# An exclusion between GpSimd and VectorE in a kernel's list scheduler, with updated durations

## The chip, the cores and the metric

The kernel runs on one core of a Trainium2 chip. The metric is the device time of one execution in microseconds, the median of several runs. Every run is a whole launch: inputs from HBM, all three stages, output to HBM.

## The reference

The reference chains three stages. The first is causal attention with a sliding window of 64 positions on 4 batches, 8 heads, 576 positions and 64 features a head. The other two are dense feed-forward blocks on the 2304 tokens of 512 features that come out, one after the other.

```python
scores = scale * np.matmul(q, k.transpose(0, 1, 3, 2))
mask = (rel >= 0) & (rel < window)          # window = 64
attn = softmax(np.where(mask, scores, -1e9))
x = np.matmul(attn, v)                       # -> 2304 tokens x 512

h = x @ w_in                                 # 512 -> 2048
g = h * np.clip(h + 3.0, 0.0, 6.0) / 6.0
x = g @ w_out                                # 2048 -> 512

h = x @ w2_in                                # the second block
g = np.maximum(0.01 * h, h)
out = g @ w2_out
```

## The kernel before

All matrix products keep high precision by splitting each operand into a rounded part (names that end in h) and a rest (names that end in l) and adding three products. The weights arrive as 64-bit numbers (tile st). A chain on ScalarE and VectorE turns each 128x512 block into 32-bit numbers (tile ca: lines 381, 370 twice, 386, 389 and the add that the profile calls CUSTOM_DVE_ANT_0 at line 342) and then into its two parts: w0h and w0l for the first product of a feed-forward block, w1h and w1l for the second. VectorE writes the l parts.

Attention works on items. Item 0 is one window of 64 queries, the others are pairs of windows, and each pair has two halves. For a half, TensorE computes scores into PSUM (L507). VectorE takes the row maximum (L466) and scales it into nb (L467, 128x4). ScalarE takes the exponential (L455). VectorE sums the rows (L476, in the first five items) and forms the reciprocal rc (L462 and L463, 128x4). GpSimd multiplies the probabilities by rc (L343, 128x512). TensorE transposes them (L532) and ScalarE copies the result, and TensorE multiplies by v (L564). The first five items run ahead of everything else. The later items are woven into the first feed-forward block.

That block begins with six column blocks f of 128 hidden features, over five token blocks. For each f, TensorE computes h (L617: twelve products in the order xs0h by w0h, xs0h by w0l, xs0l by w0h, then the same for xs1 to xs3), ScalarE and VectorE form g (r at L636 and L641, gh, gl at L645), and TensorE adds to y (L663). The rest of both feed-forward blocks uses a scheme with fewer products (lines from about 943 on).

The order of the work is not written by hand. The whole program is recorded in an object of class Order as a list of operations. Each operation has one or more ways (engine, modelled duration, function that emits it), the operations that it depends on, and a delay. `run` plays six rounds. A round is a forward pass, which starts the ready operation with the earliest due time on the engine that is free first, and a backward pass, which sets new due times. The round with the shortest modelled end wins, and its operations are emitted by modelled start time. Each engine then executes its own list in that order, so the modelled durations do nothing on the chip except set these lists. An operation with two ways (`copy`, `tensor_tensor`) may go to either engine, with a bias against the second way.

Of the kernel before, what the change touches and what calls it, by code (L numbers as in the profile page):

```python
# [17 lines left out]
class Order:  # L18
# [90 lines left out]
    def forward(self, due):  # L109


        ops, after = self.ops, self.after
        n = len(ops)
        left = [len(deps) + len(behind) for _, deps, behind, _ in ops]
        ready, free, done, start, used = {}, {}, [0.0] * n, [0.0] * n, [0] * n

        def push(i):
            ways, deps, behind, _ = ops[i]
            for k, w in enumerate(ways):
                t = 0.0  # L120
                for d in deps:
                    t = max(t, done[d] + self.lag(ops[d][0][used[d]][0], w[0]))
                for d in behind:
                    t = max(t, start[d])
                ready.setdefault(w[0], {})[i] = (t, k)

        for i in range(n):
            if not left[i]:
                push(i)
        for _ in range(n):  # L130
            while True:
                e, t = min(
                    ((e, max(free.get(e, 0.0), min(x[0] for x in q.values()))) for e, q in ready.items() if q),
                    key=lambda x: x[1],
                )
                q = ready[e]
                i = min((j for j, x in q.items() if x[0] <= t), key=lambda j: (q[j][0] if e == "DMA" else due[j], j))
                r, k = ready[e][i]
                ways, _, _, delay = ops[i]
                best = min(  # L140
                    range(len(ways)), key=lambda m: max(free.get(ways[m][0], 0.0), r, t) + ways[m][1] + self.BIAS * m
                )
                if best == k:
                    break
                del ready[e][i]
            for w in ways:
                ready.get(w[0], {}).pop(i, None)
            start[i], used[i] = max(t, r), k
            free[e] = start[i] + ways[k][1]
            done[i] = free[e] + delay  # L150
            for s in after[i] + self.then[i]:
                left[s] -= 1
                if not left[s]:
                    push(s)
        return start, used, max(done)
# [68 lines left out]
def swa_relu6_leaky_kernel(ctx: ExitStack, tc: tile.TileContext, q, k, v, w_in, w_out, w2_in, w2_out, out):  # L224
# [14 lines left out]
    nc = tc.nc  # L239
    B, _, NP, S = k.shape  # L240
# [41 lines left out]
    op = od.op  # L282

    def buf(tag, shape, dtype=F32, bufs=2):
        return od.buf(sb, shape, dtype, tag, bufs)
# [30 lines left out]
    def slot(tag, pool=None, shape=None, bufs=0):  # L316
        return od.slot(tag, pool, shape, F32, bufs, HOMES[tag])

    def act(n, fn):
        return ("ACT", 0.19 + n * 0.00083, fn)  # L320

    def dve(n, fn, fast=False):
        return ("DVE", 0.15 + n * (0.00052 if fast else 0.00104), fn)

    def pool(n, fn):
        return ("POOL", 0.2 + n * 0.0024, fn)

    def pe(t, fn):
        return ("PE", t, fn)
# [9 lines left out]
        )  # L339

    def tensor_tensor(n, dst, a, b, alu, last=True):
        d = dve(n, lambda: nc.vector.tensor_tensor(out=dst(), in0=a(), in1=b(), op=alu))  # L342
        p = pool(n, lambda: nc.gpsimd.tensor_tensor(out=dst(), in0=a(), in1=b(), op=alu))  # L343
        return (d, p) if last else (p, d)

# [3 lines left out]
    def load(bytes_, dst, src, writes, reads=(), later=()):  # L349
        op([("SP", 0.62, lambda: nc.sync.dma_start(out=dst(), in_=src))], reads, writes, later=later)  # L350
        op([("DMA", bytes_ / 3.6e5, lambda: None)], (), writes, delay=2.0)
# [10 lines left out]
    def rounded(src, later=()):  # L362

        st = buf("st", [P, DM, 2], U32, bufs=ST)
        a = buf("ca", [P, DM], U32)
        r = buf("cr", [P, DM], U32)
        load(P * DM * 8, lambda: st().rearrange("p n t -> p (n t)"), src.bitcast(U32), [st], later=later)

        def ts(dst, src, s1, s2, op0, op1=None):
            return dve(DM, lambda: nc.vector.tensor_scalar(  # L370
                out=dst(), in0=src(), scalar1=s1, scalar2=s2, op0=op0, **({"op1": op1} if op1 else {})
            ), True)

        def high():
            return st()[:, :, 1]

        def af():
            return a().bitcast(F32)

        op([  # L380
            act(DM, lambda: nc.scalar.activation(out=af(), in_=high().bitcast(F32), func=AF.Abs)),  # L381
            ts(a, high, 0x7FFFFFFF, None, ALU.bitwise_and),
        ], [st], [a])
        op([ts(af, af, EXP_LO, EXP_HI, ALU.max, ALU.min)], [a], [a])
        op([ts(a, a, 3, 0x3FFFFFFF, ALU.logical_shift_left, ALU.bitwise_and)], [a], [a])
        op([dve(DM, lambda: nc.vector.scalar_tensor_tensor(  # L386
            out=a(), in0=high(), scalar=0xC0000000, in1=a(), op0=ALU.bitwise_and, op1=ALU.bitwise_or
        ))], [a, st], [a])
        op([act(DM, lambda: nc.scalar.activation(  # L389
            out=r(), in_=st()[:, :, 0], func=AF.Copy, scale=2.0 ** -29  # L390
        ))], [st], [r])
        op(tensor_tensor(DM, a, a, r, ALU.add), [a, r], [a])
        return a, af

# [38 lines left out]
    def softmax(L, pp, early, apart):  # L433
        s = slot("s")
        nb = buf("nb", [P, NP], bufs=4)
        sm = buf("sm", [P, NP], bufs=4)
# [5 lines left out]
        def sv():  # L442
            return s()[:, :, 0:L]
# [28 lines left out]
            op([("DVE", NP * (0.23 + L * 0.00104), low)], [pp], [s, nb])  # L472
        src = [pp, nb] if early else [s, nb]
        if apart:
            op([("ACT", NP * (0.2 + L * 0.00083), exps)], src, [s])
            op([dve(NP * L, lambda: nc.vector.tensor_reduce(out=sm(), in_=sv(), axis=AX.X, op=ALU.add))], [s], [sm])  # L476
        else:
            op([("ACT", NP * (0.3 + L * 0.00083), exps)], src, [s, sm])
        op([("DVE", 0.35, recips)], [sm], [rc])
        op(tensor_tensor(NP * L, sv, sv, lambda: rc().unsqueeze(2).to_broadcast([P, NP, L]), ALU.mult, False),  # L480
           [s, rc], [s])
# [121 lines left out]
    def st_h(idx):  # L603
        b, f, first, last = steps[idx]
        o, n = blocks[b]
# [16 lines left out]
        r = buf("r", [P, 512])  # L622
        gh = buf("gh", [P, 512], F32R)
        gl = buf("gl", [P, 512], F32R)
# [7 lines left out]
        def gg():  # L632
# [5 lines left out]
                out=rr(), in0=h(), scalar1=3.0, scalar2=0.0, op0=ALU.add, op1=ALU.max  # L638
# [3 lines left out]
            out=rr(), in0=rr(), scalar=6.0, in1=h(), op0=ALU.min, op1=ALU.mult  # L642
# [1 line left out]
        op(copy(n, gg, rr, True, 1.0 / 6.0), [r], [gh])  # L644
        op([dve(n, lambda: nc.vector.scalar_tensor_tensor(  # L645
            out=gl()[:, 0:n], in0=rr(), scalar=1.0 / 6.0, in1=gg().bitcast(F32), op0=ALU.mult, op1=ALU.subtract
        ))], [r, gh], [gl])
        gs[idx] = (gh, gl)

    def st_y(idx):  # L650
# [161 lines left out]
    def paired():  # L812
# [517 lines left out]
        out=mask_f[0:W], in_=mask_f[0:W], compare_op=ALU.is_gt, fill=MASKED / SCALE, base=0,  # L1330
# [3 lines left out]
        out=mask_f[0:W], in_=mask_f[0:W], compare_op=ALU.is_ge, fill=MASKED / SCALE, base=W,  # L1334
# [47 lines left out]
    for idx in range(len(steps) + 1):  # L1382
        if idx < len(steps):
            b, f, first, last = steps[idx]
# [6 lines left out]
            for nb in range(1, NB):  # L1391
                i, n = idx - begin[nb - 1], begin[nb] - begin[nb - 1]
# [56 lines left out]
```

## Time and profile before

| | |
|---|---|
| median of 3 runs | 835.64 us (835.43 to 836.39) |
| profiled execution, its own time | 833.62 us |
| span of its instructions | 831.8 us |
| granted TensorE clock, mean | 1.000 |
| TensorE busy | 815.5 us (98%) |
| VectorE busy | 663.1 us (80%) |
| ScalarE busy | 537.9 us (65%) |
| GpSimd busy | 41.0 us (5%), 36 of its 45 instructions at L343 |

Busy time is a share of the whole span. The span has stages with different limits, so the table says which engine is full on average and not which one is waited for at a given place. The time outside the span of the profiled execution is 833.62 - 831.8 = 1.8 us. A difference of about 0.2% (1.7 us) is the least that a measurement of this kernel tells from none.

### The profile page before, as it was taken

The numbers are of one execution on the slowest core, as the hardware profiler recorded it, in microseconds if no ns is written. First come the engines' busy times: TensorE is split into PE (matmuls) and PEld (weight loads), VectorE is DVE, ScalarE is ACT, GpSimd is POOL, SyncE is SP. The second block draws the span as 40 slices with busy tenths as digits, with TensorE's granted clock in tenths as the row PEclk, the third lists the DMA queues.
The fourth block names the chain that finished last, engine by engine and source line by source line (L and its number), as shares of the span: only waits on it lengthen the run. The fifth ranks groups of instructions, "written<-read, shape, count | busy, mean of one in ns | idle before, by whom it ended". The sixth has DMA issues, their size and how long they took to land.

```text
span 831.8 us, 16109 instructions
## 1 busy us (share of the span) xinstructions
PE 815.5 (98%) x5686; PEld 747.2 (90%) x5686; DVE 663.1 (80%) x1442; ACT 537.9 (65%) x1218; POOL 41.0 (5%) x45
## 2 busy tenths in 40 slices
PE   6799999999999999999999999999999999999998
PEld 5577888888999999999999988998999999999998
DVE  6999887788757888878888867898866688866766
ACT  5988888776666666657567646877674456555541
POOL 3222221210000000000000000000000000000000
PEclk9999999999999999999999999999999999999999
DMA  7976494648685879998899875788898787987735
GB/s 240 350 271 204 130 341 152 216 153 279 226 329 191 297 265 374 326 377 300 291 378 350 301 272 203 279 285 297 283 361 265 243 255 242 308 269 238 247 127 177
DMA packets 133792, 222.32 MB, mean 267 GB/s; under 512 B 12112, under 2 KB 55632, under 8 KB 133712
## 3 DMA queue, kind: packets, MB, share of 16 engines
q1 hardware_dynamic: 133712, 221.30, 77.9%
q8 instruction: 45, 0.74, 0.4%
q14 instruction: 35, 0.29, 0.1%
HBM read 165.94 MB, written 55.31 MB: 266 GB/s over the span
## 4 chain that ended last, share of the span: by engine, by line
PE 93%; DMA 3%; DVE 2%; ACT 1%; issue 0%; SPq 0%; POOL 0%; POOLq 0%; ACTq 0%; DVEq 0%
PE h L943 28%; PE y L1211 14%; PE y L1037 10%; PE y L663 9%; PE h L617 8%; PE a L943 6%; PE y L1086 5%; PE a L1037 5%; PE a L1086 3%; PE h L564 1%; PE a L532 1%; DMA qt<-in_q_dram 1%; PE a L507 1%; DMA xd<-xa 1%; DMA xb<-in_v_dram 0%; PE y L507 0%
## 5 line engine op out<-in xcount | busy, mean ns | idle before, releaser
L943 PE MATMUL h<-e,w0l 128*128 128x384 f32 x306 | 90.4, 335 | 0.0
L943 PE MATMUL h<-e,w0h 128*128 128x384 f32 x270 | 82.0, 335 | 0.0
L1037 PE MATMUL y<-at,w1h 128*128 128x512 f32 x240 | 79.4, 391 | 0.0
L370 DVE TENSOR_SCALAR ca<-ca 128x512 uint32<-128x512 uint32 (+1 forms) x128 | 55.9, 449 | 7.8 <-ACT ca L381 6.7
L332 ACT ACTIVATE qt<-h 128x384 f32<-128x384 f32 x65 | 31.7, 488 | 45.3 <-PE h L943 44.7
L943 PE MATMUL h<-xa,w0l 128*128 128x384 f32 x204 | 59.3, 335 | 0.0
L347 DVE TENSOR_TENSOR qt<-h,qt 128x384 f32<-128x384 f32 x57 | 31.7, 556 | 32.5 <-PE h L943 18.7
L943 PEld LDWEIGHTS h<-e,w0l 128*128 128x128 f32 x306 | 56.5, 188 | 0.4
L943 PE MATMUL h<-xa,w0h 128*128 128x384 f32 x180 | 54.1, 335 | 0.0
L1037 PEld LDWEIGHTS y<-at,w1h 128*128 128x128 f32 x240 | 45.1, 188 | 8.8
L943 PEld LDWEIGHTS h<-e,w0h 128*128 128x128 f32 x270 | 50.0, 188 | 0.4
L381 ACT ACTIVATE ca<-st 128x512 f32<-128x512 f32 x64 | 42.3, 665 | 11.0 <-DMA st<-in_moe_w_out_dram 4.1
L1037 PE MATMUL a<-at,w1h 128*128 128x256 f32 x240 | 47.8, 282 | 0.0
L1037 PE MATMUL y<-at,w1l 128*128 128x512 f32 x120 | 47.2, 394 | 0.0
L389 ACT ACTIVATE cr<-st 128x512 uint32<-128x512 uint32 x64 | 42.4, 670 | 7.2 <-DMA st<-in_moe_w_out_dram 3.8
L343 POOL TENSOR_TENSOR at<-at,rc 128x512 f32<-128x512 f32 (+1 forms) x36 | 39.7, 1103 | 137.5 <-DVE rc L463 89.7
L663 PE MATMUL y<-gh,w1h 128*128 128x512 f32 (+1 forms) x120 | 45.6, 380 | 0.0
L342 DVE CUSTOM_DVE_ANT_0 ca<-ca,cr 128x1024 uint16<-128x1024 uint16 x64 | 44.8, 707 | 0.9 <-ACT cr L389 0.6
L386 DVE SCALAR_TENSOR_TENSOR ca<-st,ca 128x512 uint32<-128x512 uint32 x64 | 44.5, 701 | 0.6
L663 PE MATMUL y<-gl,w1h 128*128 128x512 f32 (+1 forms) x120 | 44.4, 370 | 0.1
L663 PE MATMUL y<-gh,w1l 128*128 128x512 f32 (+1 forms) x120 | 44.3, 369 | 0.0
L332 ACT ACTIVATE at<-qt 128x384 fp32r<-128x384 f32 x69 | 35.9, 521 | 9.3 <-DVE qt L906 6.3
(379 smaller groups left out, 2421.0 us busy)
## 6 DMA issues: line engine op xcount, KB each, us to landing
w0h<-kept SPq DMA_DIRECT2D x116, 256.0 KB, 4.4
w0l<-kept SPq DMA_DIRECT2D x115, 256.0 KB, 4.4
w1h<-kept SPq DMA_DIRECT2D x76, 256.0 KB, 4.2
w1l<-kept SPq DMA_DIRECT2D x76, 256.0 KB, 4.4
st<-in_moe_w_in_dram SPq DMA_DIRECT2D x32, 512.0 KB, 6.2
st<-in_moe_w_out_dram SPq DMA_DIRECT2D x32, 512.0 KB, 5.1
kept<-e SPq DMA_DIRECT2D x33, 256.0 KB, 3.9
kept<-gh SPq DMA_DIRECT2D x30, 256.0 KB, 4.9
```

The costliest lines, as they stand in the source:

```text
L332: a = act(n, lambda: nc.scalar.activation(out=dst(), in_=src(), func=AF.Copy, scale=scale))
L342: d = dve(n, lambda: nc.vector.tensor_tensor(out=dst(), in0=a(), in1=b(), op=alu))
L370: return dve(DM, lambda: nc.vector.tensor_scalar(out=dst(), in0=src(), scalar1=s1, scalar2=s2, op0=op0, **({"op1": op1} if op1 else {})), ...
L381: act(DM, lambda: nc.scalar.activation(out=af(), in_=high().bitcast(F32), func=AF.Abs)),
L386: op([dve(DM, lambda: nc.vector.scalar_tensor_tensor(out=a(), in0=high(), scalar=0xC0000000, in1=a(), op0=ALU.bitwise_and, op1=ALU.bitwise ...
L389: op([act(DM, lambda: nc.scalar.activation(out=r(), in_=st()[:, :, 0], func=AF.Copy, scale=2.0 ** -29))], [st], [r])
L617: nc.tensor.matmul(ph()[:, 0:n], wt()[:, cs], xt()[:, 0:n], start=(c == 0 and m == 0), stop=(c == NK - 1 and m == 2),)
L663: nc.tensor.matmul(y()[:, 0:n], stat()[:, cs], mov()[:, 0:n], start=(first and m == 0), stop=(last and m == 2))
L943: nc.tensor.matmul(bk()[:, 0:HT], a, b_(), start=(start and j == 0 and q_ == 0), stop=(j == 1 and q_ == 2), skip_group_check=True,)
L1037: nc.tensor.matmul(y()[:, d:d + n], a()[:, cs], b_[1]()[:, t0:t0 + n], start=(begins and m == 0), stop=(last and m1 and m == 2), skip_grou ...
L1086: nc.tensor.matmul(y(), a()[:, cs], b_(), start=(first and m == 0), stop=(last and m == 2))
L1211: nc.tensor.matmul(y()[:, 256 * k:256 * k + 256], a()[:, cs], b_, start=(start and k == 0 and e == 0 and q_ == 0), stop=(e == 1 and q_ == ...
```

## The change

The forward pass gains a rule: an operation whose way carries a fourth entry may not start on VectorE while such an operation runs on GpSimd, and the other way round. GpSimd operations carry the mark, and so do VectorE operations with two SBUF inputs or with the factor for fast one-input operations. The small operations on nb and rc (L467, L462, L463) and the operations that read PSUM carry none. Modelled durations change too: a GpSimd product of 512 columns goes from 0.2 + 512 * 0.0024 = 1.43 us to 0.19 + 512 * 0.00168 = 1.05 us, and the fixed part of an exponential from 0.2 or 0.3 us to 0.18 or 0.24 us.

```diff
+        port = {"DVE": 0.0, "POOL": 0.0}
+
+        def at(i, x):
+            w = ops[i][0][x[1]]
+            return max(x[0], port["POOL" if w[0] == "DVE" else "DVE"]) if len(w) > 3 else x[0]
...
-                    ((e, max(free.get(e, 0.0), min(x[0] for x in q.values()))) for e, q in ready.items() if q),
+                    ((e, max(free.get(e, 0.0), min(at(j, x) for j, x in q.items()))) for e, q in ready.items() if q),
...
-                i = min((j for j, x in q.items() if x[0] <= t), key=lambda j: (q[j][0] if e == "DMA" else due[j], j))
-                r, k = ready[e][i]
+                i = min((j for j, x in q.items() if at(j, x) <= t), key=lambda j: (q[j][0] if e == "DMA" else due[j], j))
+                k = ready[e][i][1]
+                r = at(i, ready[e][i])
...
             free[e] = start[i] + ways[k][1]
+            if len(ways[k]) > 3:
+                port[e] = free[e]
...
-    def dve(n, fn, fast=False):
-        return ("DVE", 0.15 + n * (0.00052 if fast else 0.00104), fn)
+    def dve(n, fn, fast=False, port=False):
+        way = ("DVE", 0.15 + n * (0.00052 if fast else 0.00104), fn)
+        return (*way, True) if fast or port else way
 
     def pool(n, fn):
-        return ("POOL", 0.2 + n * 0.0024, fn)
+        return ("POOL", 0.19 + n * 0.00168, fn, True)
...
-            op([("ACT", NP * (0.2 + L * 0.00083), exps)], src, [s])
+            op([("ACT", NP * (0.18 + L * 0.00083), exps)], src, [s])
...
-            op([("ACT", NP * (0.3 + L * 0.00083), exps)], src, [s, sm])
+            op([("ACT", NP * (0.24 + L * 0.00083), exps)], src, [s, sm])
```

The mark `port=True` is also given to the VectorE way of `tensor_tensor` (L342), to L386 and to L645. Every engine executes the same instructions as before, the same number of each, and GpSimd's list is the same in the same order. What changes is the order on the other queues: the maximum, sum and reciprocal operations of the first items, the weight conversions between them, and with them places on TensorE, ScalarE and the DMA queue. In the stages after the first six column blocks the lists differ by neighbours that change places. All line numbers of the changed kernel are 9 higher at the places shown here.

The first place is VectorE's list at the end of the first five items (nb and y are the row maxima of a half, sm its sums, rc its reciprocals, ca a weight block under conversion). Before:

```order
L466 TENSOR_REDUCE nb<-y_251 128x4
L467 TENSOR_SCALAR nb<-nb 128x4
L462 TENSOR_SCALAR rc<-sm 128x4
L463 RECIPROCAL rc<-rc 128x4
L476 TENSOR_REDUCE sm<-at 128x4
L466 TENSOR_REDUCE nb<-y_270 128x4
L467 TENSOR_SCALAR nb<-nb 128x4
L462 TENSOR_SCALAR rc<-sm 128x4
L463 RECIPROCAL rc<-rc 128x4
L476 TENSOR_REDUCE sm<-at 128x4
L370 TENSOR_SCALAR ca<-ca 128x512
L462 TENSOR_SCALAR rc<-sm 128x4
```

After, at the same place of the program:

```order
L471 TENSOR_SCALAR rc<-sm 128x4
L472 RECIPROCAL rc<-rc 128x4
L485 TENSOR_REDUCE sm<-at 128x4
L471 TENSOR_SCALAR rc<-sm 128x4
L472 RECIPROCAL rc<-rc 128x4
L485 TENSOR_REDUCE sm<-at 128x4
L471 TENSOR_SCALAR rc<-sm 128x4
L472 RECIPROCAL rc<-rc 128x4
L485 TENSOR_REDUCE sm<-at 128x4
L471 TENSOR_SCALAR rc<-sm 128x4
L472 RECIPROCAL rc<-rc 128x4
L379 TENSOR_SCALAR ca<-ca 128x512 x2
```

The row maxima have moved ahead, the weight conversion has moved behind the last reciprocal, and between two reciprocals there is one sum where there were a sum and another operation of 512 columns.

The second place is VectorE's list where item 5's reciprocal stands, ahead of the second column block's w0l. Before:

```order
L342 ISA ca<-ca,cr 128x1024
L462 TENSOR_SCALAR rc<-sm 128x4
L463 RECIPROCAL rc<-rc 128x4
L370 TENSOR_SCALAR ca<-ca 128x512 x2
L342 TENSOR_TENSOR w0l<-ca,w0h 128x512
L466 TENSOR_REDUCE nb<-a 128x4
L467 TENSOR_SCALAR nb<-nb 128x4
```

After:

```order
L471 TENSOR_SCALAR rc<-sm 128x4
L472 RECIPROCAL rc<-rc 128x4
L351 ISA ca<-ca,cr 128x1024
L379 TENSOR_SCALAR ca<-ca 128x512
L650 SCALAR_TENSOR_TENSOR r<-r,h 128x512
L475 TENSOR_REDUCE nb<-a 128x4
L476 TENSOR_SCALAR nb<-nb 128x4
L351 TENSOR_TENSOR w0l<-ca,w0h 128x512
```

The add of the second block (ISA) now stands behind the reciprocal, and w0l behind r and a row maximum, both of which read PSUM.

The third place is VectorE's list at the next reciprocal (item 6's first half). Before:

```order
L386 SCALAR_TENSOR_TENSOR ca<-st,ca 128x512
L462 TENSOR_SCALAR rc<-sm 128x4
L463 RECIPROCAL rc<-rc 128x4
L342 ISA ca<-ca,cr 128x1024
L641 SCALAR_TENSOR_TENSOR r<-r,h 128x512
L645 SCALAR_TENSOR_TENSOR gl<-r,gh 128x512
```

After:

```order
L379 TENSOR_SCALAR ca<-ca 128x512
L471 TENSOR_SCALAR rc<-sm 128x4
L472 RECIPROCAL rc<-rc 128x4
L379 TENSOR_SCALAR ca<-ca 128x512
L395 SCALAR_TENSOR_TENSOR ca<-st,ca 128x512
L379 TENSOR_SCALAR ca<-ca 128x512
L351 ISA ca<-ca,cr 128x1024
```

Where one marked operation and one that reads PSUM stood behind the reciprocal, there are now marked operations alone.

## Rows read from the trace of the kernel before

**Rows 1.** The page: span, and busy time by engine

```profile
span 831.8 us, 16109 instructions
PE 815.5 (98%) x5686; PEld 747.2 (90%) x5686; DVE 663.1 (80%) x1442; ACT 537.9 (65%) x1218; POOL 41.0 (5%) x45
```

**Rows 2.** Windows: stretch, length, busy us of PE, PEld, DVE, ACT, POOL, clock, DMA

```profile
21.00:42.00 21.00, 16.38 (x191) 11.60 (x191) 19.50 (x44) 19.30 (x55) 4.45 (x5) 1.00 1.02 353
42.00:62.00 20.00, 19.31 (x182) 14.90 (x182) 19.72 (x43) 17.83 (x58) 4.70 (x4) 1.00 0.74 274
62.00:83.00 21.00, 20.03 (x191) 16.00 (x190) 19.65 (x57) 18.53 (x53) 4.84 (x4) 1.00 0.62 202
83.00:800.00 717.00, 717.00 (x4689) 665.94 (x4688) 569.87 (x1221) 461.47 (x1003) 20.29 (x18) 1.00 0.80 272
```

**Rows 3.** Waits of TensorE's weight loads, 20 to 80 us: total us, times, longest

```profile
PEld h L532 <- POOL at L343: 2.8, 3, 1.4
PEld h L617 <- DVE w0l L342: 2.7, 4, 1.3
```

**Rows 4.** Timeline of VectorE and GpSimd, 14 to 18 us: start, us, instruction

```profile
14.44 0.16 DVE L462 TENSOR_SCALAR rc<-sm 128x4 f32<-128x4 f32 x1
14.64 0.18 DVE L463 RECIPROCAL rc<-rc 128x4 f32<-128x4 f32 x1
14.96 1.04 POOL L343 TENSOR_TENSOR at<-at,rc 128x512 f32<-128x512 f32 x1 [0.41 <-DVE rc L463]
15.43 0.60 DVE L467 TENSOR_SCALAR nb<-nb 128x4 f32<-128x4 f32 x1
16.82 0.68 DVE L466 TENSOR_REDUCE nb<-y 128x4 f32<-128x512 f32 x1
17.54 0.17 DVE L467 TENSOR_SCALAR nb<-nb 128x4 f32<-128x4 f32 x1
```

**Rows 5.** Timeline at the third place, 43 to 46 us

```profile
43.64 0.66 DVE L342 CUSTOM_DVE_ANT_0 ca<-ca,cr 128x1024 uint16<-128x1024 uint16 x1
43.89 1.31 POOL L343 TENSOR_TENSOR at<-at,rc 128x512 f32<-128x512 f32 x1 [6.01 <-DVE rc L463]
44.22 0.68 DVE L641 SCALAR_TENSOR_TENSOR r<-r,h 128x512 f32<-128x512 f32 x1
44.82 0.93 DVE L645 SCALAR_TENSOR_TENSOR gl<-r,gh 128x512 fp32r<-128x512 f32 x1
```

**Rows 6.** Timeline, 48 to 51 us

```profile
48.75 0.66 DVE L645 SCALAR_TENSOR_TENSOR gl<-r,gh 128x512 fp32r<-128x512 f32 x1
49.01 1.31 POOL L343 TENSOR_TENSOR at<-at,rc 128x512 f32<-128x512 f32 x1 [3.81 <-DVE rc L463]
49.33 1.27 DVE L370 TENSOR_SCALAR ca<-ca 128x512 f32<-128x512 f32 x1
```

**Rows 7.** Timeline at the second place, 33 to 39 us

```profile
33.04 0.42 DVE L370 TENSOR_SCALAR ca<-ca 128x512 f32<-128x512 f32 x1
...
37.01 1.15 DVE L370 TENSOR_SCALAR ca<-ca 128x512 f32<-128x512 f32 x2
37.26 0.61 POOL L343 TENSOR_TENSOR at<-at,rc 128x256 f32<-128x256 f32 x1 [9.85 <-DVE rc L463]
38.08 0.68 DVE L342 TENSOR_TENSOR w0l<-ca,w0h 128x512 fp32r<-128x512 f32 x1
38.81 0.50 PE L617 MATMUL h<-xs0h,w0l 128*128 128x512 f32 x1 [0.37 <-DVE w0l L342]
```

**Rows 8.** Timeline ahead of the fifth column block, 64 to 68 us

```profile
64.78 2.49 POOL L343 TENSOR_TENSOR at<-at,rc 128x512 f32<-128x512 f32 x2 [8.16 <-ACT w1h L332]
64.80 1.57 DVE L342 TENSOR_TENSOR w1l<-ca,w1h 128x512 fp32r<-128x512 f32 x1
66.30 1.52 DVE L342 TENSOR_TENSOR w0l<-ca,w0h 128x512 fp32r<-128x512 f32 x1
67.87 0.50 PE L617 MATMUL h<-xs0h,w0l 128*128 128x512 f32 x1 [0.97 <-DVE w0l L342]
```

More of the change, by code (lines that the diff above doesn't have):

```diff
@@ L341, in tensor_tensor @@
     def tensor_tensor(n, dst, a, b, alu, last=True):
-        d = dve(n, lambda: nc.vector.tensor_tensor(out=dst(), in0=a(), in1=b(), op=alu))
+        d = dve(n, lambda: nc.vector.tensor_tensor(out=dst(), in0=a(), in1=b(), op=alu), port=True)
         p = pool(n, lambda: nc.gpsimd.tensor_tensor(out=dst(), in0=a(), in1=b(), op=alu))
@@ L387, in rounded @@
             out=a(), in0=high(), scalar=0xC0000000, in1=a(), op0=ALU.bitwise_and, op1=ALU.bitwise_or
-        ))], [a, st], [a])
+        ), port=True)], [a, st], [a])
         op([act(DM, lambda: nc.scalar.activation(
@@ L646, in st_h @@
             out=gl()[:, 0:n], in0=rr(), scalar=1.0 / 6.0, in1=gg().bitcast(F32), op0=ALU.mult, op1=ALU.subtract
-        ))], [r, gh], [gl])
+        ), port=True)], [r, gh], [gl])
         gs[idx] = (gh, gl)
```

## The prediction

> **What bounds the kernel now.** I read the page first. TensorE is busy for 98% of the span and no other engine for more than 80% [rows 1]. Busy shares are averages over stages, so the windows come next. From 83 to 800 us TensorE is busy for all 717 of 717 us [rows 2]. Nothing that another engine does there can be seen in the time, unless it grows by more than VectorE's spare 717 - 570 = 147 us. Before that it is different. From 21 to 42 us TensorE works 16.4 of 21.0 us, while VectorE works 19.5 and ScalarE 19.3. From 42 to 62 us VectorE works 19.7 of 20.0 us, from 62 to 83 us 19.7 of 21.0 [rows 2]. So VectorE paces the kernel from about 9 to 70 us, and TensorE the rest. The waits say the same: between 20 and 80 us TensorE's weight loads wait 2.8 us for GpSimd's normalised probabilities and 2.7 us for w0l, which VectorE writes [rows 3].
>
> The timeline shows what the change is about. The scaling of nb takes 0.17 us at 17.54 us, but 0.60 us at 15.43 us, where it ends with the GpSimd product that began at 14.96 us and takes 1.04 us [rows 4]. The two engines exclude each other, and an operation of 128x4 is held as well. What I call a hold is the time by which an operation runs longer for this reason, here 0.60 - 0.17 = 0.43 us.
>
> A second rule can be read from three more places. A GpSimd product that becomes ready while a VectorE operation runs waits for that one alone: its row is then 1.31 us long, and the VectorE operation behind is held [rows 5, 6]. At 49.33 us a conversion step takes 1.27 us in place of 0.42 us, a hold of 0.85 us [rows 6, 7]. Where an operation that reads PSUM stands second, such as r at 44.22 us, it takes its usual 0.68 us, and only the third is held, by 0.93 - 0.68 = 0.25 us [rows 5].
>
> **The change part by part.** The new durations emit nothing. They alter the lists only, and the value for GpSimd is now the measured one (1.05 us in the model, 1.04 us in the trace [rows 4]). No instruction is added, removed or given to another engine, so the work costs the same. The DMAs are the same too, and the q load of the fifth item moves ahead of a weight block. I cost that at nothing, because VectorE's list and not the load decides when that item's maxima can be taken. The swaps of neighbours behind 83 us cost nothing either, with TensorE full above them [rows 2]. Without that cover, a swap costs at most one operation of VectorE, 0.68 us.
>
> What remains is the first 70 us, and there the sum is the holds in VectorE's list, before and after, because that engine has no slack. Before, I count eleven up to the end of the fifth column block's w0l. The first is the one at 15.43 us (0.43) and the last the one at 66.30 us (0.84) [rows 4, 8]. By stretch they are 2.10 us up to 28 us, 0.30 at the second place, 0.25 at the third, 2.29 between 49 and 57 us, and 0.89 + 0.84 at w1l and w0l at 64 to 68 us. Together they make 6.67 us.
>
> After, I place GpSimd's products along the new list with the same rows.
>
> In the start-up, a product begins 0.32 us after its reciprocal does (14.64 to 14.96 us) and is over 1.04 us later, at 1.36 us [rows 4]. In the new list a sum follows the reciprocal. It starts at 0.09 us, and the next rc operation comes 0.60 us behind, at 0.69 us. It would be followed at 0.89 us. It is held to 1.36 us, ends at 1.39 and is followed at 1.44 us, a hold of 0.55 us. The list has that pattern three times in a row where it had two operations of 512 columns in between, so 1.65 us. Two scalings of nb further up meet a product in the same way, for 0.15 and 0.44 us. The pair of conversion steps behind the last reciprocal gives 0.85 us, as in [rows 6]. The sum is 3.09 us against 2.10 us. The holds and waits of this stretch partly cover each other, but the weight conversions, which used to fill VectorE between the reciprocals, now begin behind them, so I let nothing go.
>
> At the second place the hold is the same 0.30 us (1.15 us for a pair that takes 0.85 us [rows 7]). But w0l now stands behind r and a maximum, so TensorE, which today waits 0.37 us for it at 38.81 us [rows 7], will wait about 2 us. Queued behind that wait are the other products of h for this column block, then y. Most of it comes back, because r, the maxima and gl are then ready earlier, and TensorE's next waits are for those. I count nothing here and keep 1.6 us as the upper bound.
>
> At the third place the operation behind the first marked one is now a marked one in place of r. So the hold is 0.85 us and not 0.25 us [rows 5, 6].
>
> In the next reciprocals I find a scaling of nb held for 0.36 us, a small rc operation for 0.89 us and a conversion step for 0.85 us, 2.10 us against 2.29 us. At the fifth column block there are two holds of 0.85 us, against 0.89 and 0.84 us.
>
> The sum after is 3.09 + 0.30 + 0.85 + 2.10 + 1.70 = 8.04 us. The difference to 6.67 us is +1.37 us. The last of these operations is a w0l that TensorE waits for (67.87 us, 0.97 us idle ahead of it [rows 8]), so it should appear in the end in full. Against the profiled execution's own 833.62 us that gives 835.0 us. The runs shown have a median of 835.64 us, 2.0 us above it, so the forecast for a median is 837.0 us.
>
> The bounds of the unknown part are those of the seven small holds (0.15, 0.44, three times 0.55, 0.36 and 0.89, together 3.49 us). Below, none of them is held. Then the list has 4.55 us of holds against 6.67, a gain of 2.1 us, of which I let 0.3 us go to ScalarE's exponentials, which the last sums would then wait for. That leaves -1.8 us. Above, each is held for nearly a whole product, 0.95 us. That makes 6.65 us in place of 3.49 and +4.5 us in all. I take the value between them because [rows 4] shows a small operation held to the end of the product and no further.
>
> The Trainium skill bears on exactly this (SBUF — State Buffer, section Who interferes with whom). It says that one-input operations such as tensor_scalar can take the port pair that VectorE shares with GpSimd, that the pair is locked for a whole instruction, and that the loser is blocked entirely. The trace agrees, 0.60 against 0.17 us. By that rule the small operations on nb and rc belong to the excluded ones, and the marks of the change leave them out. If the marks were complete and these were free, the sum would be the -1.8 us above.
>
> **The rivals.**
>
> *The order avoids the holds (faster).* One mechanism: the small operations slip past GpSimd's products, because a product starts late by ScalarE's exponentials, and the row maxima then stand under it unheld, as r does at 44.22 us [rows 5]. The price is that of the lower bound, 833.8 us. If in addition the product ahead of the fifth column block is through before w1l, another 0.85 us goes and it is 833.0 us. It decides once the small holds total less than 2.1 us, which is 3.49 - 1.37. That the model now uses GpSimd's measured duration speaks for it. Against it speaks that the list puts seven small operations where a product runs.
>
> *The change doesn't show.* The lists differ only in their first part, and holds lost at one reciprocal come back at another, as in the last two pairs of sums above. The median stays at 835.6 us, give or take 0.5 us. For it speaks that the number of products and of marked operations is the same. Against it, the three equal patterns in a row.
>
> *The wait for the second column block's w0l is not given back (slower by more).* TensorE then keeps the 1.6 us of the second place on top of the 1.4 us, which makes 838.6 us. For it speaks that eleven more products of h stand behind the one that waits. Against it, TensorE waits today for r, gl and the exponentials right behind it.
>
> **How the numbers follow.** I give the forecast 0.48, the faster rival 0.28, no change 0.13 and the slower rival 0.11. The forecast's own range is 835.8 to 838.2 us. With the limit of 0.2% (1.7 us, so 834.0 and 837.3 us), I split the forecast into 0.28 within and 0.20 slower, and the faster rival into 0.22 faster and 0.06 within. That gives faster 0.22, same 0.28 + 0.06 + 0.13 = 0.47, slower 0.20 + 0.11 = 0.31. The range reaches down to the faster rival's lowest value, 833.0 us, and up past the slower rival to 839.0 us. It leaves out some 0.18.
>
> **What would show it.** In the new profile the rc operations (L471) between 20 and 26 us should take about 0.7 us where they take 0.16 us now. The operation behind the first marked one at the third place should take 1.5 us. TensorE should wait some 2 us for the second column block's w0l, and the fifth block's w0l should end about 1.4 us later than 67.8 us. From 83 us on TensorE should be full again. The forecast is wrong if VectorE is idle for long in the first 30 us, because then holds fall into waits. It is also wrong if TensorE shows a new wait after 83 us, or if GpSimd's products start so much later or earlier that the patterns don't meet.

## The result

The changed kernel takes 841.8 us, the median of 5 runs (838.53 to 842.59), against 836.39 us for the kernel before beside it (835.43 to 838.96). The ratio is 1.0065, 95% interval 1.0046 to 1.0084: slower by 5.4 us, or 0.65%. The forecast was 837.0 us, with a range up to 839.0 us. The profiled execution took 842.59 us, the longest of the five, and the one before 833.62 us, below all the runs beside it, so the two profiles lie 9.0 us apart, more than the medians.

The page's first rows and the windows of the profile after, with the columns of [rows 1, 2]:

```profile
span 840.8 us, 16099 instructions
PE 816.5 (97%) x5686; PEld 748.3 (89%) x5686; DVE 663.5 (79%) x1442; ACT 539.3 (64%) x1218; POOL 40.5 (5%) x45
...
21.00:42.00 21.00, 13.66 (x179) 10.34 (x179) 16.40 (x36) 16.50 (x42) 5.34 (x6) 0.92 1.00 340
42.00:62.00 20.00, 17.36 (x177) 13.41 (x174) 19.42 (x41) 17.17 (x54) 4.64 (x5) 1.00 0.58 190
62.00:83.00 21.00, 20.21 (x187) 15.73 (x186) 19.38 (x52) 19.20 (x57) 3.39 (x3) 1.00 0.72 239
83.00:800.00 717.00, 714.23 (x4650) 661.60 (x4649) 568.30 (x1225) 463.34 (x1010) 21.56 (x19) 1.00 0.80 272
```

Every engine does the same work as before. The surprise is in the first window. VectorE, which was to be busier there with holds, works 16.4 us in place of 19.5 [rows 2], and ScalarE 16.5 in place of 19.3. Both wait. TensorE loses 2.7 us there, 2.0 us in the next window and 2.8 us behind 83 us, where it was full before.

The waits of TensorE between 14 and 40 us (instruction, what it waited for, total us, times, longest) name the place:

```profile
PE a L573 <- DMA xb<-in_v_dram: 4.5, 1, 4.5
PE h L541 <- POOL at L352: 2.4, 3, 1.0
PE y L516 <- DMA qt<-in_q_dram: 1.5, 1, 1.5
```

The product with v (PV) of the fifth item waits 4.5 us for its v load. In the kernel before that item's PV had waited 1.30 us, for ScalarE. The timelines of the load queue (SPq) and of that PV show why. First before:

```profile
22.65 0.62 SPq L350 DMA_DIRECT2D qt<-in_q_dram  x1
23.37 0.92 SPq L350 DMA_DIRECT2D xb<-in_v_dram  x1
24.39 0.38 SPq L350 DMA_DIRECT2D at<-in_v_dram  x1
26.91 0.55 SPq L350 DMA_DIRECT2D xb<-in_k_dram  x1
29.30 0.54 SPq L350 DMA_DIRECT2D xb<-in_k_dram  x1
29.42 0.69 PE L564 MATMUL a<-at,xb 128*64 128x64 f32 x16 [1.30 <-ACT xa L332]
```

Then after:

```profile
22.43 0.62 SPq L359 DMA_DIRECT2D qt<-in_q_dram  x1
23.09 1.45 SPq L359 DMA_DIRECT2D xb<-in_k_dram  x2
24.64 2.04 SPq L359 DMA_DIRECT2D xb<-in_v_dram  x1
26.78 0.51 SPq L359 DMA_DIRECT2D at<-in_v_dram  x1
32.99 1.12 PE L573 MATMUL a<-at,xb 128*64 128x64 f32 x16 [4.55 <-DMA xb<-in_v_dram]
```

Two k loads of 384 KB each, for later items (TensorE first uses them at 59.5 us), now stand ahead of the v load. It is issued 1.3 us later (24.64 against 23.37 us) and lands 8.2 us after its issue, against 5.9 us before. The k loads' 768 KB take about 2.1 us at the 368 GB/s that this stretch moves (an estimate from the windows below), close to the 2.3 us between the two.

The wait has a second price. The windows of the profile after, in the same columns:

```profile
28.00:30.00 2.00, 0.45 (x4) 0.21 (x2) 1.97 (x5) 1.84 (x4) 0.00 (x0) 1.00 1.11 368
30.00:32.00 2.00, 0.00 (x0) 0.00 (x0) 1.72 (x3) 0.95 (x3) 0.00 (x0) 1.00 1.05 391
...
33.00:34.00 1.00, 1.00 (x19) 1.00 (x21) 0.11 (x1) 0.00 (x0) 0.00 (x0) 0.50 1.10 248
34.00:35.00 1.00, 1.00 (x20) 0.88 (x16) 0.00 (x0) 0.00 (x0) 0.00 (x0) 0.50 1.02 283
35.00:36.00 1.00, 1.00 (x12) 0.78 (x13) 0.00 (x0) 0.96 (x3) 0.00 (x0) 0.50 1.03 254
```

After 4.5 us without work TensorE comes back at a granted clock of 0.50, its lower level of 1.2 GHz, for over 3 us. The same 16 products of PV take 1.12 us where they took 0.69 us.

The holds that the forecast was made of are there too. VectorE and GpSimd after, at the second reciprocal of the row of three:

```profile
23.58 1.04 POOL L352 TENSOR_TENSOR at<-at,rc 128x512 f32<-128x512 f32 x1 [0.41 <-DVE rc L472]
24.03 0.61 DVE L471 TENSOR_SCALAR rc<-sm 128x4 f32<-128x4 f32 x1
24.68 0.18 DVE L472 RECIPROCAL rc<-rc 128x4 f32<-128x4 f32 x1
```

The rc operation takes 0.61 us, in place of 0.16 us in [rows 4], at three places. The other places that the forecast named, from the timeline after (the wait for the second block's w0l, the marked operation behind the third place's reciprocal, and the fifth block's w0l):

```profile
44.54 0.50 PE L626 MATMUL h<-xs0h,w0l 128*128 128x512 f32 x1 [1.59 <-DVE w0l L351]
...
46.73 1.53 DVE L395 SCALAR_TENSOR_TENSOR ca<-st,ca 128x512 uint32<-128x512 uint32 x1
...
71.35 1.53 DVE L351 TENSOR_TENSOR w0l<-ca,w0h 128x512 fp32r<-128x512 f32 x1
```

Summed over VectorE's instructions up to 76 us (each one's time less the median of its form, where that is over 0.05 us) the holds are 6.64 us before and 7.34 us after.

### The profile page after: what moved, and what is told of

It is laid out like the page before. It is cut to its first block, busy times and chain, and to the rows that moved or that the text cites. A ratio compares the mean times of both kernels' runs of the same rounds, so it can differ in the third digit from the quotient of the medians.

```text
span 840.8 us, 16099 instructions
## 1 busy us (share of the span) xinstructions
PE 816.5 (97%) x5686; PEld 748.3 (89%) x5686; DVE 663.5 (79%) x1442; ACT 539.3 (64%) x1218; POOL 40.5 (5%) x45
## 4 chain that ended last, share of the span: by engine, by line
PE 91%; DMA 4%; DVE 3%; ACT 2%; issue 1%; SPq 0%; POOL 0%; POOLq 0%; DVEq 0%
PE h L952 27%; PE y L1220 14%; PE y L1046 10%; PE y L672 8%; PE h L626 8%; PE a L952 6%; PE a L1046 5%; PE y L1095 5%; PE a L1095 2%; DMA xb<-in_v_dram 2%; PE h L573 1%; PE a L541 1%; PE a L516 1%; DMA qt<-in_q_dram 1%; DMA st<-in_moe_w_out_dram 1%; PE a L573 1%
```

## The experiments

Theory A: the order of the load queue costs the time. Theory B, the forecast's: the holds cost it. Theory C: the swaps of neighbours in the later part do. Most kernels below plan twice, with the old durations and no rule (list o0, rank r0, times s0) and with the new durations and the rule (o1, r1, s1). Every operation goes to the same engine in both plans. `merge` emits the operations so that each engine's list follows the rank given for it. So one queue's order can be taken from one plan and the rest from the other. The ratios are to the kernel before, run beside each; brackets hold 95% intervals.

**Queue and lists exchanged.**

```diff
-        for i in sorted(range(n), key=lambda i: (start[i], i)):
+        order = self.merge(o1, used, {**{e: r1 for e in ("PE", "DVE", "ACT", "POOL", "DMA")}, "SP": r0, "DMA": r0})
+        for i in order:
```

> The changed lists of TensorE, VectorE, ScalarE and GpSimd, with the load queue (SP) in the order of the kernel before. Theory A (the new queue lets two k loads go ahead of the v loads, and TensorE waits for a v load): the 4.5 us wait of PV for xb<-in_v_dram is gone, what stays there is at most 1.5 us, and the time is 3.0 to 4.5 us below the changed kernel, so within 0.2% to 0.35% of before. Theory B (the holds by GpSimd products, as predicted): the order of the loads does not matter, the time is that of the changed kernel, 0.65% above before, give or take 0.15%.

Measured: 838.25 us, ratio 1.0041 [1.0028, 1.0054], 3.7 us above before. The v load is issued at 25.33 us, and TensorE's wait for it is 2.0 us. Both lie a little above what theory A had (0.35% and 1.5 us), and the ratio below theory B's 0.5%.

```diff
+        order = self.merge(o0, used, {**{e: r0 for e in ("PE", "DVE", "ACT", "POOL")}, "SP": r1, "DMA": r1})
```

> The engine lists of the kernel before, with only the load queue (SP) in the changed order. Theory A: TensorE waits 3 to 5 us for a v load near 28 us and the time is 3.0 to 5.0 us above before (0.35% to 0.6%). Theory B: no difference, within 0.15% of before, because the lists of VectorE and GpSimd are the old ones.

Measured: 841.66 us, ratio 1.0081 [1.0065, 1.0097]. That is more than theory A's 0.6%. The wait for xb<-in_v_dram is 4.2 us. VectorE's list is the old one and its holds are 6.58 us, so theory B cannot make this loss. The queue's order alone can. But the first run says that the new lists also cost something on their own.

**The program cut in two**, at about 94 us of the trace.

```diff
+        head = [i for i in o1 if s1[i] < 90]
+        h = set(head)
+        order = head + [i for i in o0 if i not in h]
```

> All queues in the changed order up to about 90 us of the program, in the old order behind it. Theory A: the loss is in the head, so the time stays 4.5 to 6.5 us above before (0.55% to 0.8%). Theory C (neighbour swaps in the later part, where the changed kernel's profile has waits of 2.1 us at 495 us and 0.6 us at 577 us, cost half of the loss): 2.0 to 3.5 us above before (0.25% to 0.4%).

Measured: 841.87 us, 1.0086 [1.0068, 1.0103]. With the two plans exchanged (head of o0, rest of o1):

> All queues in the old order up to about 90 us of the program, in the changed order behind it. Theory A: within 0.1% of before. Theory C: 2 to 3.5 us above before (0.25% to 0.4%), with the waits for qt in the second half of the program in the profile.

Measured: 836.18 us, 1.0011 [1.0000, 1.0021]. The loss is in the head. Theory C falls as the main cause, though the tail is not quite free.

**The two k loads alone.** Operations 293 and 349 are the issues of these loads, 115 and 117 those of the fifth item's v loads.

```diff
+        rank = dict(r1)
+        rank[293], rank[349] = r1[117] + 0.3, r1[117] + 0.6
+        order = self.merge(o1, used, {..., "SP": rank, ...})
```

> The changed kernel with one move in the load queue: the two k loads into xb stand behind the v loads of the fifth item in place of ahead of them, everything else on every queue as changed. Theory A in its narrow form (these two loads alone delay the v load): the wait for xb<-in_v_dram falls from 4.5 us to about 2 us and the time comes to the level of the run with the whole old queue, 0.3% to 0.45% above before. Rival (the other moves of the queue carry the loss): 0.6% to 0.8% above before.

Measured: 839.27 us, 1.0032 [1.0019, 1.0045], as theory A has it: half of the loss goes with one move in one queue. In its profile, taken at 836.99 us, the least of its twelve, TensorE does not wait for the v load. The converse, with `rank = dict(r0)` and the two set to r0[115] - 0.6 and - 0.3 in the old lists:

> The kernel before with one move in the load queue: the two k loads into xb ahead of the v loads of the fifth item. Theory A in its narrow form: most of the 7.1 us that the whole new queue cost the old lists comes back, 4 to 7 us above before (0.5% to 0.85%), with a wait of 4 us or more for xb<-in_v_dram near 29 us. Rival (other moves of the queue): at most 2 us above before (0.25%).

Measured: 839.5 us, 1.0036 [1.0022, 1.0051], 3.4 us above before. That is short of the expected 4 us. The wait is there in full, as the line of TensorE's waits shows:

```profile
PE a L618 <- DMA xb<-in_v_dram: 4.7, 1, 4.7
```

These two loads carry about half of what the whole new queue cost the old lists (0.81%). Which other moves carry the rest was not tried.

**The order of the loads mended in the planner, and all holds modelled.**

```diff
-        late_ = [loads[KHOLD]] if len(tiles) >= 4 and len(loads) > KHOLD else []
+        hold = KHOLD + 2 if len(tiles) >= 6 else KHOLD
+        late_ = [loads[hold]] if len(tiles) >= 4 and len(loads) > hold else []
```

> The change, with the k loads of the seventh item on held behind the ninth v load in place of the seventh; the scheduler then makes its own lists. Theory A: the wait for xb<-in_v_dram is 2 us or less and the time is 0.1% to 0.45% above before. Theory B (the holds): the lists of VectorE and GpSimd meet as in the changed kernel, 0.6% to 0.8% above before.

Measured: 837.07 us, 1.0013 [0.9998, 1.0027]. Then with the small operations marked as well:

```diff
-        op([("DVE", 0.35, recips)], [sm], [rc])
+        op([("DVE", 0.35, recips, True)], [sm], [rc])
```

> As the run with the k loads held, and the small operations on nb and rc marked too (the scaling of nb is an operation of its own for that), so that the model counts every hold that the trace shows. Theory B: the 3.5 us of small holds are gone, and the time is 2 to 4 us below the run with the k loads held, at or below before. Theory A: what is left has little to do with the holds, within 1 us of the run with the k loads held.

Measured: 838.08 us, 1.0023 [1.0007, 1.0039], not below the run before it. Its holds are 6.17 us against 6.46 us there. So the completed marks shortened the holds by little and the kernel not at all, and the run does not test theory B, which asked for 3.5 us less of holds.

**GpSimd's products cut to a quarter**, in the old lists and in the new ones with the old queue.

```diff
-        op(tensor_tensor(NP * L, sv, sv, lambda: rc().unsqueeze(2).to_broadcast([P, NP, L]), ALU.mult, False),
+        part = lambda: s()[:, :, 0:L // 4]
+        op(tensor_tensor(NP * L, part, part, lambda: rc().unsqueeze(2).to_broadcast([P, NP, L // 4]), ALU.mult, False),
```

> All lists of the kernel before, with each GpSimd product on a quarter of its columns (the normalisation of the other three quarters is left out), so that a hold can be at most about 0.4 us. Theory B and theory A alike: some 3 to 6 us below before, because TensorE's 2.8 us of waits for these products and the holds shrink. It is the base for the next run.

Measured: 835.03 us, 0.9990 [0.9974, 1.0006].

> The changed lists of TensorE, VectorE, ScalarE and GpSimd with the old load queue, and the products cut to a quarter as in the run before. With whole products these lists cost 3.7 us more than the old ones. Theory B (that difference is made of holds): at most 1.2 us above the old lists with the cut products. Rival (the new lists lose by their order alone, as at the wait for w0l of the second column block): still 2.5 to 4.5 us above them.

Measured: 836.6 us, 1.0004 [0.9986, 1.0021]. The holds up to 76 us are down to 0.41 and 0.80 us. The expectation of the first run was wrong: 6.2 us of holds are gone from the old lists, and the time falls by 0.9 us, within the interval of nothing. The difference between the two, 1.6 us, lies between the theories, and its interval (each ratio is good to 0.16%) holds both.

**The two parts of the change, one at a time.** Durations without the rule, `self.lists(1, 0, rounds)`:

> The new durations alone, without the rule on GpSimd and VectorE. The queue keeps the v loads of the fifth item ahead of the two k loads. Theory A: within 0.35% of before. Theory B (the rule's lists make the holds): within 0.15% of before, as the lists come without the rule.

Measured: 838.84 us, 1.0034 [1.0021, 1.0047]. The rule without the durations, `self.lists(0, 1, rounds)`:

> The rule alone, with the old durations. Theory A: the time goes by the place of the two k loads, which stand ahead of one or both v loads of the fifth item if the model lets TensorE free the v slot late: then 0.4% to 0.8% above before, otherwise within 0.35%. Theory B: the holds decide, 0.2% to 0.5% above before.

Measured: 839.31 us, 1.0034 [1.0021, 1.0047]. In both, one of the two k loads stands ahead of the v loads, not none as I had written for the first. TensorE waits 2.5 and 3.3 us for the v load. Either part alone makes about half of the loss. The engine lists of each are new as well, so what of it is the queue's is not shown. The ratio of the rule alone lies in theory B's range and just below theory A's.

**What is left in the new lists.** With the k loads behind, w0h and w0l of the second column block moved ahead (operations 178 and 179, on ScalarE and VectorE):

```diff
+        act[178], dve[179] = r1[166] - 0.5, r1[167] - 0.5
```

> As the run with the two k loads behind (3.1 us above before), and in addition the second column block's w0h moved ahead of one operation on ScalarE and its w0l ahead of r and a row maximum on VectorE, as in the old lists. If the wait for w0l is one of the costs that are left: TensorE's wait there falls from 1.4 us to 0.7 us or less and the time by 0.7 to 1.3 us, to 0.2% to 0.3% above before. If it is given back later: no difference from the run with the two k loads behind.

Measured: 838.91 us, 1.0041 [1.0025, 1.0057], no gain. TensorE waits 0.23 us for w0l in place of 1.15 us in the run with the k loads behind, and then waits at the transposes that follow:

```profile
40.67 0.50 PE L674 MATMUL h<-xs0h,w0l 128*128 128x512 f32 x1 [0.23 <-DVE w0l L399]
...
43.92 0.60 PE L589 MATMUL a<-ident_r,at 128*64 128x128 f32 x4 [1.14 <-issue]
```

From the 11th to the 61st product of 512 columns this kernel takes 19.87 us. The one with the k loads behind takes 19.95 us, but at a granted clock of 0.50 in part of that stretch (from about 34.3 to 37.6 us). The run with the new lists and the old queue leaves w0l at its changed place, waits 1.41 us for it and, at a clock of 1.00 like the first, takes 19.35 us. So the shorter wait is not seen in the stretch; what the transposes waited for the profile does not name ("issue"). With the old order behind 94 us instead:

> As the run with the two k loads behind, with all queues in the old order from about 90 us of the program on. If neighbour swaps in the later part cost what the traces show (one wait of 0.6 us near 571 us in each kernel with the changed tail): 0.4 to 1.0 us below the run with the two k loads behind. If they cost nothing, as predicted: no difference.

Measured: 838.67 us, 1.0049 [1.0030, 1.0068], no gain in the median. The wait near 571 us is gone. The runs spread from 836.7 to 843.7 us, so 0.6 us cannot be told.

**The v loads ahead of all k and q loads**, in the old and in the new lists:

```diff
+        for n, i in enumerate((115, 117)):
+            rank[i] = r0[142] - 0.8 + 0.3 * n
```

> The kernel before with the fifth item's two v loads ahead of the two k and two q loads that stood in front of them. If the landing of these v loads bounds the start-up in the old kernel too: the first product of h starts 1 to 2 us earlier and the time falls by 1 to 2 us (0.12% to 0.25%). If only the chain of GpSimd products and their holds bounds it: no difference (within 0.1%).

Measured: 836.87 us, 1.0014 [1.0000, 1.0028], no gain. TensorE no longer waits there, but it then waits 1.2 and 0.8 us for xs0h and xs1h, the split values that the last PV ends in. The second of these stands on ScalarE behind a conversion step that waits 1.06 us for a weight load.

> The changed kernel with the fifth item's v loads ahead of all six k and q loads that stood in front of them, everything else as changed. If the v landing is what the two k loads delay: at or below the run with the two k loads behind, 0.15% to 0.35% above before. Rival: the k and q loads of the sixth item land late in its place, and the time stays 0.5% to 0.8% above before.

Measured: 844.58 us, 1.0107 [1.0088, 1.0125]. The rival holds, above even its range of 0.8%. Among the waits of TensorE between 2 and 90 us are these two, and ScalarE's timeline shows what stands ahead of xs2h:

```profile
PE h L671 <- ACT xs2h L386: 4.0, 1, 4.0
...
PE a L561 <- DMA qt<-in_q_dram: 1.6, 1, 1.6
...
40.73 0.66 ACT L435 ACTIVATE ca<-st 128x512 f32<-128x512 f32 x1 [5.29 <-DMA st<-in_moe_w_in_dram]
41.29 0.61 ACT L386 ACTIVATE xs2h<-xa 128x512 fp32r<-128x512 f32 x1
```

The larger wait is for a weight load, which the rival did not name, and the smaller one for a q load, as it had it. In both lists, what was moved ahead made another load late.

**The cut at 75 us**, with the k loads behind in the first kernel:

```diff
-        head = [i for i in o1 if s1[i] < 90]
+        head = [i for i in o1 if s1[i] < 72]
```

> As the run with the two k loads behind (0.32% above before), with all queues in the old order from about 75 us of the program on. If the later part costs what the rows show (a wait of 0.6 us near 88 us with 0.3 us beside it, and 0.75 us near 571 us): 1.2 to 2.0 us less than the run with the two k loads behind, 0.08% to 0.2% above before. If the later swaps cost nothing, as predicted: still 0.3% above before.

Measured: 840.34 us, 1.0064 [1.0039, 1.0090], a miss. Its runs go from 836.6 to 842.9 us, and in its profile the first PV, which frees the slot for the next v loads, starts at 16.73 us, against 14.45 us in the run with the k loads behind. The two profiles were taken at 841.82 and 836.99 us, the latter the least of that kernel's twelve, so the difference may be one of executions.

> The old order on all queues up to about 75 us, the changed order behind it. If the later part costs what the rows show: 1.2 to 2.0 us above before (0.15% to 0.25%), with the waits near 88 and 571 us in the profile. If the later swaps cost nothing, as predicted: within 0.1% of before.

Measured: 836.54 us, 1.0021 [1.0008, 1.0034], 1.8 us above before, as expected. Its timeline shows both places:

```profile
84.11 0.60 PE L586 MATMUL a<-ident_r,at 128*128 128x128 f32 x4
84.64 0.33 PE L618 MATMUL h<-at 128*64 128x64 f32 x2
84.74 0.60 ACT L386 ACTIVATE at<-a 128x512 f32<-128x512 f32 x1 [0.46 <-PE a L586]
85.39 1.15 PE L618 MATMUL h<-at 128*64 128x64 f32 x30 [0.43 <-ACT at L386]
...
568.40 0.62 ACT L386 ACTIVATE w0h<-st 128x512 fp32r<-128x512 f32 x1
568.92 0.51 ACT L386 ACTIVATE at<-r 128x384 fp32r<-128x384 f32 x1
569.33 0.47 ACT L386 ACTIVATE qt<-h 128x384 f32<-128x384 f32 x1
569.86 0.44 PE L997 MATMUL h<-e,w0h 128*128 128x384 f32 x1 [0.43 <-ACT qt L386]
```

In the first, four transposes stand right ahead of the PV that needs their copy. The old list has them ahead of twelve products of h, which cover the copy. In the second, ScalarE takes w0h and at ahead of qt; before, w0h came earlier and qt ahead of at. Neither is a hold.

## Why the prediction was wrong

**The step that failed first** is the sentence on the DMAs: "The DMAs are the same too, and the q load of the fifth item moves ahead of a weight block. I cost that at nothing". The loads are the same, their order is not. I named one move of the queue and left out the one that mattered: two k loads ahead of the fifth item's v loads. Moved alone they cost the old lists 3.4 us (0.36%), and moved back alone they leave the new ones at 0.32% in place of 0.65%. The DMA share of that stretch was 1.02 before [rows 2]. In a queue that is full a move can have a price, and I did not ask for it; none of the rivals did either. The Trainium skill (SBUF — State Buffer, section A bandwidth-pool intuition that's wrong (but worth ruling out)) gives about 358 GB/s between HBM and one core. The trace differs: the windows here show 368 and 391 GB/s, and the measurement decides. That the transfers had little room left is read from the DMA share of 1.11 and 1.05 in the same windows.

Why the planner moved them: a load's issue waits there only for its slot, and the queue takes what is ready. In the new plan the slot of the v load frees a little after the queue is idle, so the k loads, which are wanted much later, go first. Their hold (KHOLD) is tied to the seventh v load, not the ninth. Tying it to the ninth, with all lists planned anew, leaves 0.13%, which is not told from none.

**The second step that failed** is "because that engine has no slack", from which every hold counted in full. The holds themselves were read rightly: 6.67 us before by hand and 6.64 us by the sum over all instructions. After, 8.04 us were forecast and 7.34 us measured. Each rc hold is 0.45 us where 0.55 us was worked out, and the small ones are 2.8 us together where 3.49 us was. But 6.2 us of holds taken out of the old lists are worth 0.9 us, by the interval at most 2.2 us. So the 0.7 us by which the holds grew can't make the loss, and that the forecast had the right sign is luck. A busy share of 93% in a window [rows 2] is no proof that the engine paces it: in the start-up the loads do as well, as the two k loads show. The range, too, was narrower than its own working. The upper bound of +4.5 us on the median of 835.64 us is 840.1 us, and the range ended at 839.0 us. The measured +5.4 us lies above both.

**"The swaps of neighbours behind 83 us cost nothing"** failed too, by 1.8 us. In eight profiles with the new later part, the stretch from the start of the 1001st product of 512 columns to the end of the span is 336.9 to 337.0 us; in eight with the old one it is 336.1 to 336.2 us. The stretch from the 121st to the 181st grows from 19.5 to 20.4 us, with whole products and with quarters alike. Full busy time in [rows 2] hid that TensorE was full because its list had the covers in place. The price named for a swap without cover, 0.68 us, was near in size: the two stretches grow by 0.9 and 0.8 us, of which TensorE's products stand idle for 0.43 us each. But it was named for an operation of VectorE, and these are transposes of TensorE and copies of ScalarE.

**A step that was missing**: TensorE's own list. The new one takes the scores of an item ahead of item 0's transposes, and these scores wait for a q load. Transposes, scores and first PV before:

```profile
11.72 0.63 PE L532 MATMUL h<-ident_r,at 128*64 128x128 f32 x4 [0.43 <-POOL at L343]
12.85 1.10 PE L507 MATMUL y<-xb,qt 64*64 64x128 f32 x32 [0.28 <-DMA qt<-in_q_dram]
14.31 0.68 PE L564 MATMUL a<-at 64*64 64x64 f32 x16
```

Scores, transposes and first PV after:

```profile
13.76 1.10 PE L516 MATMUL y<-xb,qt 64*64 64x128 f32 x32 [1.52 <-DMA qt<-in_q_dram]
14.79 0.63 PE L541 MATMUL h<-ident_r,at 128*64 128x128 f32 x4
16.10 0.68 PE L573 MATMUL a<-at 64*64 64x64 f32 x16 [0.44 <-ACT at L341]
```

The first PV starts at 16.10 us, against 14.31 us before, and with it the slot for the next v load comes free later. In the profiles with the new head it starts at 14.5 to 17.7 us, in those with the old one at 14.3 to 15.3 us. This would fit the spread of the runs with the new head, which is not shown: no run changed TensorE's list alone.

**What was right.** The rc operations took 0.61 us where "about 0.7 us" was foreseen, and the operation behind the first marked one at the third place 1.53 us where 1.5 us was. TensorE waits 1.6 us for the second column block's w0l (2 us foreseen), and shortening that wait was no gain in the run with w0l ahead, so the rival that it is not given back finds no support; the reason that the prediction gave for it was not shown. By the Trainium skill (SBUF — State Buffer, section Who interferes with whom) operations such as the tensor_scalar on nb and rc can contend with GpSimd. The trace agrees: they are held, 0.60 and 0.61 us in place of 0.17 and 0.16 us. But a complete set of marks was no gain (0.23% above before, against 0.13%). Two signs that the prediction named against itself came, in part: TensorE has new waits behind 83 us, and VectorE stands nearly idle, though from 33 to 36 us and not in the first 30. The fifth block's w0l was forecast 1.4 us later and ends 5.1 us later, at 72.88 us.

**What stays open.** The new lists cost 0.3% to 0.4% without the two k loads. Put behind the old head, the new later part costs 0.2%, and the stretches named above give 1.7 us for it. But the two runs that took it away from the new head were not faster (0.49% and 0.64% above before, against 0.32%), so the parts don't simply add up. The rest is in the start-up. One piece of it can be placed: from the 11th to the 61st product of 512 columns the old lists take 18.59 and 18.60 us with the old and the new queue, and the new lists 19.35 and 19.33 us, all four at a granted clock of 1.00. The others, TensorE's first PV, holds, loads and the granted clock, were not divided further. The granted clock may take part: its mean over the twelve runs with the two k loads ahead is 0.9951, over those of the kernel before beside them 0.9969. By an estimate from these, 0.0018 of 840 us, up to some 1.5 us of their 3.4 us may be clock. The profiled execution after has a wait of TensorE of 1.9 us more at 497 us, where ScalarE waits 4.8 us for a weight load. Such waits of TensorE, 0.6 to 1.9 us behind a late weight, come and go near 322, 418 and 495 us in kernels with old and new lists, so it is not laid to the change. No version run here is faster than the kernel before beyond its interval.

## What to carry to other kernels

When a scheduler's numbers change, compare the load queue's list first, load by load, and ask of each load that moved what is behind it and when that is wanted. Before counting a hold in full, find what waits for its end: in a start-up where loads, TensorE and VectorE are each over 90% busy in turn, a gain on one is taken by the next. A late list change on a full engine is free only while its covers stay ahead of it.

## What the hardware showed that I had not expected

A wait of TensorE can cost more than its length. After 4.5 us of idleness its granted clock was 0.50 for over 3 us, and 16 products took 1.12 us in place of 0.69 us. Such stretches are common here: 18 of the 20 profiles have one or two between 12 and 50 us, 3.4 or 6.8 us in all (worked out from windows of 2 us), and only the profile before and that of the last run have none. Of the 124 runs of the kernel before beside the experiments, the 46 with a mean granted clock of 0.999 or more have a median of 834.5 us, the 25 with 0.995 or less one of 836.8 us. And the landing of the first q loads is not the same from kernel to kernel though they are issued alike: the second, issued at 2.7 to 2.8 us, lands 5.0 to 7.6 us later. TensorE's waits for them in the first 20 us are 1.2 to 3.6 us in these profiles, and whatever hangs on the first PV moves with it.
